# Attention's transfers leave one by one behind ScalarE's operations, and the first expert's weights in halves

## Chip, cores and metric

The kernel runs on one core of a Trainium2 chip. The metric is device time in microseconds, the median of several runs. A trace belongs to one profiled execution, whose span (first to last instruction) is a little shorter than that execution's own time.

## What is computed

Attention over 8 batches and 8 heads, with 512 local and 32 global positions of dimension 64. A local query sees the local keys within 32 positions and all global keys; a global query sees everything. The 4608 rows of 512 then go through a mixture of 16 experts in 4 groups, one expert per row.

```python
s_ll = np.where(np.abs(pos[:, None] - pos[None, :]) <= 32, scale * q_l @ k_l.T, -1e9)
a_l = sm(concat([scale * q_l @ k_g.T, s_ll]))
out_l = a_l @ concat([v_g, v_l])
out_g = sm(scale * q_g @ k_all.T) @ v_all
x = rows of (out_g, out_l)                      # 4608 x 512
g = argmax(x @ w_group); e = argmax(x @ w_expert[g])
out[row] = softmax weights of g and e * (relu(x[row] @ w1[g, e]) @ w2[g, e])
```

## The kernel before

The kernel has two stages. **Attention** walks a list of 40 items, numbered by `n`: for each batch `b` four tiles of 128 local queries, (b, 0) to (b, 3), and one item (b, 'g') for the global queries. Within batches 0 to 6 the global item comes last, so item 4 is (0, 'g') and item 5 is (1, 0). **The experts** follow: for each of 16 experts rows are gathered, multiplied by split weights and scattered.

The order of the engines in attention is written out by hand in the loop over `items` (L920 on); items overlap. In a pass `n` the loop emits, for the item itself, the first half of the scores on TensorE (`scores(it, 0)`, tile `s_ps`), its softmax (`softmax(it, 0)`: VectorE adds the mask into `pr` and takes the minimum, ScalarE takes the exponential, L388), the second half of the scores and of the softmax, and the transposes and the copy of the first half (`transp`, `pt_copy(it, 0)`, ScalarE, L419). For item n-1 it emits the second copy, the products with V (`pv`, tile `x_ps`, L438) and the division (`norm`, into `xbuf`, name `xb`). For items n-2 and n-3 it emits the router's products (`xtrans`, `lt_mm`, `sel_mm`, tiles `xt` and `lm`) and the store `put_x(n-3)`. GpSimd copies windows of V (`make_v`, tiles `vw`) and scatters token numbers (`put`, into `ids_d`).

All direct transfers leave on SyncE's queue (SP) in the order in which the loop emits them. One that has to wait, for a free buffer or for its data, holds those behind it. There are eight semaphores for them, DMAHW0 to DMAHW7, used in turn, so that a transfer also waits until the one eight places ahead has landed. In pass `n` SP gets, all at the head of the pass and before any compute of it:

- `put_x(n-3)`: 256 KB of `xb` to `x_all` (four pieces of 16 KB for a global item), L759 or L464
- `load_q(n+2)`: 256 KB (128 KB for a global item) into one of three buffers (`qz`, or in `kv`), L232
- pieces of the next batch's K (384 KB each, four a batch, into `k_odd` or `kv`, L238) and V (260 KB each and one of 130 KB, six a batch, L247 and L249); batch 1's come in passes 2 to 5
- from two passes after the first expert is known, one 512 KB piece of its first weights (`raw`) in each of four passes, and in passes 35 to 38 one of its second weights (into `kv`), L143

SP isn't tied to the pass in which a transfer is written: it sends as soon as the wait of the transfer allows.

Of the kernel before, what the change touches and what calls it, by code (L numbers as in the profile page):

```python
# [14 lines left out]
AF = mybir.ActivationFunctionType  # L15
# [55 lines left out]
def build(ctx, tc, qT, kT, vU, w1, w2, mask, ca, cb, out):  # L71
# [60 lines left out]
    perm = []  # L132

    def load_w(e, part, ii=range(4), behind=None):
        if e >= NE:
            return
        for i in ii:
            if part == 0:
                hf, c2 = divmod(i, 2)
                src = w1r[ds(perm[e], 1), :, 2 * c2:2 * c2 + 2, hf * 512:(hf + 1) * 512]  # L140
            else:
                src = w2r[ds(perm[e], 1), :, 2 * i:2 * i + 2, :]
            ins = SP.dma_start(out=raws[4 * part + i], in_=src.rearrange("o p c f -> (o p) c f"))  # L143
            if behind is not None:
                tc.add_manual_dep(ins.ins, behind.ins.name,
                                  mybir.DependencyInfo(mybir.DependencyClass.Sync, mybir.DependencyReason.DATA),
                                  reason="paced behind compute")
                behind = None

# [86 lines left out]

    def load_k(b, p):
        SP.dma_start(out=kbuf(b)[:, p, :], in_=kT[b, :, p, :])  # L238

# [3 lines left out]

    def load_v(b, ss):
        for s in ss:
            if s < 5:
                SP.dma_start(out=v0[b % 2][:, s, :], in_=vU[b, 128 * s:128 * s + 128, :])  # L247
            else:
                SP.dma_start(out=v0[b % 2][64:128, s, :], in_=vU[b, 640:704, :])  # L249

# [110 lines left out]
    def softmax(it, i):  # L361
# [3 lines left out]
        if t == 'g':  # L365
            if i:
                return
            mx = sm.tile([128, 2, 2], F32, name="gmx")
            nm = sm.tile([128, 2], F32, name="gnm")
            V.tensor_reduce(mx[:, :, 0], s_ps[:, :, 0:480], AX.X, ALU.max)  # L370
            V.tensor_reduce(mx[:, :, 1], g_ps.rearrange("p (h c) -> p h c", h=2), AX.X, ALU.max)
            V.tensor_reduce(nm, mx, AX.X, ALU.max)
            V.tensor_scalar(nm, nm, -0.125, None, ALU.mult)
            for h in range(2):
                A.activation(pg[h][:, 704:768], g_ps[:, 64 * h:64 * h + 64], AF.Exp, bias=nm[:, h:h + 1], scale=0.125)
            for h in range(2):
                A.activation(pg[h][:, 0:640].rearrange("p (a c) -> p a c", c=128)[:, :, 0:96],
                             s_ps[:, h, 0:480].rearrange("p (a c) -> p a c", c=96), AF.Exp, bias=nm[:, h:h + 1], scale=0.125)
            return
        if i == 0:  # L380
# [3 lines left out]
        for h in range(4 * i, 4 * i + 4):  # L384
            par, p = h % 4 // 2, 2 * i + h % 2
            V.tensor_tensor_reduce(out=pr[:, h, :], in0=s_ps[:, par, 128 * p:128 * p + 128], in1=mask_sb[:, t, :], scale=-0.125, scalar=3.0e38, op0=ALU.add,  # L386
                                   op1=ALU.min, accum_out=nm[:, h:h + 1])
            A.activation(pr[:, h, :], pr[:, h, :], AF.Exp, bias=nm[:, h:h + 1], scale=-1.0)  # L388

# [18 lines left out]
    def pt_copy(it, i):  # L408
# [3 lines left out]
        if t == 'g':  # L412
            V.tensor_copy(ptg[:, i, 0:3, :], tp[0])
            A.copy(ptg[:, i, 3:6, :], tp[1])
            return
# [3 lines left out]
        A.copy(dst, tp)  # L419

# [331 lines left out]

    def put_x(it):
        b, t = it
# [3 lines left out]
        r0 = b * S + SG + 128 * t  # L758
        SP.dma_start(out=x_all[r0:r0 + 128, 0:DM], in_=xbuf[b][:, t, :])  # L759

# [70 lines left out]

    def fetch():
        perm.append(nc.values_load(first_i[0:1, 0:1], engines=(mybir.EngineType.SP,), min_val=0, max_val=NE - 1))
        load_w(0, 0, (0,))

# [76 lines left out]
    def at(n, f, *a):  # L912
        if 0 <= n < len(items):
            f(items[n], *a)

# [4 lines left out]
    for n, it in enumerate(items):  # L920
        now[0] = n
        at(n - 3, put_x)
        if n:
# [3 lines left out]
        b1 = n // 5 + 1  # L927
        if b1 == 1:
            for p in ((), (), (0, 1), (2,), (3,))[n]:
                load_k(1, p)  # L930
            load_v(1, ((), (), (), (0, 1), (2, 3))[n])
        elif b1 < B:
            for p in ((0, 1), (2,), (3,), (), ())[n % 5]:
                load_k(b1, p)
            load_v(b1, ((), (0,), (1,), (2, 3), (4, 5))[n % 5])
        if n == 5:
            load_v(1, (4, 5))
        if chosen and n == chosen[0] + 2:
            fetch()
        elif chosen and chosen[0] + 2 < n < chosen[0] + 6:  # L940
            load_w(0, 0, (n - chosen[0] - 2,))
        if n == 31:
            early_id()
        if 35 <= n < 39:
            load_w(0, 1, (n - 35,))
        while stores and stores[0][0] <= n:
# [27 lines left out]
        if it[1] != 'g':  # L974
            rt_at(n - 2, lt_mm)
        softmax(it, 1)
        at(n - 1, norm)
# [5 lines left out]
        if it[1] == 'g':  # L983
            rt_at(n - 2, lt_mm)
        pt_copy(it, 0)
        if it[1] == 'g':
# [562 lines left out]
```

## Time and profile before

| | us |
|---|---|
| median of 3 runs | 745.93 (745.5 to 746.29) |
| the profiled execution | 743.79 |
| its span | 742.0 |
| TensorE busy | 677.9 (91% of the span) |
| VectorE, ScalarE, GpSimd busy | 410.5, 386.7, 252.0 |

Attention takes about the first 255 us, the experts the rest. The share of busy time is an average over both; what bounds a stretch is read from that stretch. An idle time put down to "issue" is one in which the engine waited for nothing that the profile shows: all semaphores that the next instruction needs were there. The DMA views list the queues: q1 carries the direct transfers that SP issues, q0 GpSimd's indirect ones, q8 and q14 instructions.

### The profile page before, as it was taken

The page shows a single profiled execution, that of the slowest core. Times are in us where ns is not written, and L with a number is a line of the kernel's source. Part 1 is how long each engine was busy: PE and PEld are TensorE (multiplying, and loading weights), DVE is VectorE, ACT ScalarE, POOL GpSimd, SP SyncE. Part 2 cuts the span into 40 slices and gives each one's busy share as a digit, 9 for nine tenths or more (in the row PEclk, how much of TensorE's full clock was granted, in tenths as well). Part 3 has the DMA queues.
Part 4 walks back from the last instruction along what each step waited for, and adds up shares of the span by engine and source line. Part 5 has one row for each costly group of instructions (what it writes and reads, how often), then busy time and mean ns, then how long its engine had stood idle before and what let it go on. Part 6 is the DMA issues. An engine that isn't in the chain of part 4 may idle for free. (4 is left out here: it accounts for less than half of the span.)

```text
span 742.0 us, 24040 instructions
## 1 busy us (share of the span) xinstructions
PE 677.9 (91%) x8891; PEld 532.2 (72%) x8891; DVE 410.5 (55%) x1360; ACT 386.7 (52%) x835; POOL 252.0 (34%) x309
## 2 busy tenths in 40 slices
PE   6889888897887989999989999999999999897996
PEld 3666566575665687767779888867886798786964
DVE  3568667686777725634265455426435563656642
ACT  4676676674757425533355344435335454545642
POOL 5534454455444463212321231232122213323211
PEclk9999999998999999999999999999999999998999
DMA  9876675676662156445348447423834464575730
GB/s 297 239 217 214 187 220 159 193 216 192 207 201 79 35 165 223 154 134 198 118 147 285 153 151 251 152 98 117 294 118 157 141 230 160 179 273 172 253 135 27
DMA packets 76279, 132.47 MB, mean 179 GB/s; under 512 B 17310, under 2 KB 21286, under 8 KB 75952
## 3 DMA queue, kind: packets, MB, share of 16 engines
q1 hardware_dynamic: 66512, 110.92, 45.9%
q0 software_dynamic: 9440, 17.94, 7.5%
q8 instruction: 113, 1.85, 1.1%
q14 instruction: 214, 1.75, 0.8%
HBM read 119.07 MB, written 19.04 MB: 186 GB/s over the span
## 5 line engine op out<-in xcount | busy, mean ns | idle before, releaser
L1183 POOL DMA_INDIRECT xg<-x_all,ids x61 | 72.5, 1189 | 249.4 <-PE yp L1252 48.6
L172 DVE TENSOR_TENSOR w1l<-raw,w1h 128x1024 fp32r<-128x1024 f32 x44 | 51.9, 1221 | 112.2 <-ACT w1h L171 112.2
L388 ACT ACTIVATE pr<-pr,nm 128x128 f32<-128x128 f32 x256 | 81.9, 391 | 48.2 <-DVE nm L386 47.9
L60 POOL COPY vw<-v 32x520 f32<-32x520 f32 (+1 forms) x112 | 69.1, 619 | 87.2 <-DMA ids_d<-cb_sb,si 44.8
L386 DVE CUSTOM_DVE_ANT_0 pr<-s_ps,mask_sb 128x128 f32<-128x128 f32 x256 | 59.0, 286 | 40.9 <-PE s_ps L357 38.6
L1277 PE MATMUL h_ps<-xTh,w1h 128*128 128x256 f32 (+5 forms) x216 | 69.5, 334 | 0.0
L1278 PE MATMUL h_ps<-xTh,w1l 128*128 128x256 f32 (+5 forms) x216 | 68.9, 331 | 0.0
L171 ACT CAST w1h<-raw 128x1024 fp32r<-128x1024 f32 x44 | 43.9, 1047 | 39.1 <-issue 39.1
L1290 DVE SCALAR_TENSOR_TENSOR hTl<-h_ps,hTh 128x256 fp32r<-128x256 f32 (+3 forms) x54 | 28.9, 535 | 56.0 <-ACT hTh L1289 50.9
L1266 PE MATMUL yqp<-w2h,hTh 128*128 128x512 f32 x128 | 52.8, 412 | 7.7 <-issue 7.7
L172 DVE TENSOR_TENSOR w2l<-kv,w2h 128x1024 fp32r<-128x1024 f32 x35 | 42.6, 1223 | 25.8 <-ACT w2h L171 17.6
L1252 PE MATMUL yp<-w2h,hTh 128*128 128x512 f32 x136 | 54.8, 403 | 0.6 <-ACT yr L1246 0.6
L1254 PE MATMUL yp<-w2h,hTl 128*128 128x512 f32 x136 | 53.9, 396 | 0.0
L1253 PE MATMUL yp<-w2l,hTh 128*128 128x512 f32 x136 | 53.9, 396 | 0.0
L1266 PE MATMUL yqp<-w2l,hTh 128*128 128x512 f32 x128 | 51.6, 403 | 0.0
L1289 ACT ACTIVATE hTh<-h_ps 128x256 fp32r<-128x256 f32 (+3 forms) x54 | 25.5, 472 | 46.8 <-PE h_ps L1283 40.2
L419 ACT COPY pt<-t_ps 128x512 f32<-128x512 f32 x64 | 36.8, 575 | 22.9 <-PE t_ps L405 22.7
L438 PE MATMUL x_ps<-v,pt 128*32 128x65 f32 x768 | 44.9, 228 | 4.1 <-ACT pt L419 2.9
L438 PE MATMUL x_ps<-vw,pt 128*32 128x65 f32 x1280 | 44.9, 228 | 2.4 <-ACT pt L419 1.1
L1283 PE MATMUL h_ps<-xTl,w1h 128*128 128x256 f32 (+5 forms) x216 | 45.4, 332 | 0.0
L1269 ACT ACTIVATE y<-yp,gt 128x512 f32<-128x512 f32 x17 | 11.7, 690 | 63.5 <-PE yp L1254 63.5
L405 PE MATMUL t_ps<-ident,pr 128*128 128x128 f32 x256 | 42.7, 290 | 1.7 <-issue 1.7
(259 smaller groups left out, 1647.0 us busy)
## 6 DMA issues: line engine op xcount, KB each, us to landing
raw<-w SPq DMA_DIRECT2D x64, 512.0 KB
kv<-w SPq DMA_DIRECT2D x64, 512.0 KB
v<-vU SPq DMA_DIRECT2D x40, 260.0 KB
x_all<-xb SPq DMA_DIRECT2D x32, 256.0 KB
k_odd<-kT SPq DMA_DIRECT2D x16, 384.0 KB
kv<-qT SPq DMA_DIRECT2D x21, 256.0 KB
kv<-kT SPq DMA_DIRECT2D x12, 384.0 KB
qz<-qT SPq DMA_DIRECT2D x11, 256.0 KB
```

Of the source, the lines that this page charges most:

```text
L60: r = op(*a, **k)
L172: V.tensor_tensor(lo, src, hi.bitcast(F32), ALU.subtract)
L386: V.tensor_tensor_reduce(out=pr[:, h, :], in0=s_ps[:, par, 128 * p:128 * p + 128], in1=mask_sb[:, t, :], scale=-0.125, scalar=3.0e38, op0= ...
L388: A.activation(pr[:, h, :], pr[:, h, :], AF.Exp, bias=nm[:, h:h + 1], scale=-1.0)
L438: P.matmul(x_ps[32 * jj:32 * jj + 32, i, DV * (h % 4):DV * (h % 4) + DV], d['pt'][:, hp, 32 * jj:32 * jj + 32], wins[(b,) + win(4 * t + jj ...
L1183: return G.indirect_dma_start(out=dst, out_offset=None, in_=x_all, in_offset=bass.IndirectOffsetOnAxis(ap=ix.bitcast(U32), axis=0), bounds ...
L1252: P.matmul(yp, hT[0][:, f, sl], w2h[f], start=(f == 0), stop=False)
L1253: P.matmul(yp, hT[0][:, f, sl], w2l[f], start=False, stop=False)
L1254: P.matmul(yp, hT[1][:, f, sl], w2h[f], start=False, stop=(f == 7))
L1266: P.matmul(yqp, hT[i][:, f, sl], w, start=(k == 0), stop=(k == 23))
L1277: P.matmul(hp[:, sl], w1h[par][:, c, fs], xT[0][:, c, sl], start=(c == 0), stop=False)
L1278: P.matmul(hp[:, sl], w1l[par][:, c, fs], xT[0][:, c, sl], start=False, stop=False)
```

## The change

A helper `pace(ins, behind)` makes a transfer wait for an operation of an engine. `softmax` and `pt_copy` now return their last ScalarE operation. In a pass `n`:

- `load_q(n+2)` stays at the head.
- V and K pieces, and weights, are put into a list `more`. `send(1, ...)` takes one out behind the exponentials of the item's first half, one behind those of the second half (not in a global item), and `send(9, ...)` all that is left behind `pt_copy(it, 0)`.
- `put_x(n-3)` comes behind `pt_copy(n-1, 1)`; in a global item it comes at that place without a wait on ScalarE.
- A 512 KB piece of the first expert's weights becomes two of 256 KB (`load_w_half`), in the same passes as before.
- Batch 1's pieces stay in passes 2 to 5, at the new places.

```diff
+    def pace(ins, behind):
+        if behind is not None:
+            tc.add_manual_dep(ins.ins, behind.ins.name,
+                              mybir.DependencyInfo(mybir.DependencyClass.Sync, mybir.DependencyReason.DATA),
+                              reason="paced behind compute")
+    def load_w_half(i, c, behind):
+        if i < 4:
+            hf, c2 = divmod(i, 2)
+            src = w1r[ds(perm[0], 1), :, 2 * c2 + c, hf * 512:(hf + 1) * 512]
+        else:
+            src = w2r[ds(perm[0], 1), :, 2 * (i - 4) + c, :]
+        pace(SP.dma_start(out=raws[i][:, c, :], in_=src.rearrange("o p f -> (o p) f")), behind)
...
     for n, it in enumerate(items):
         now[0] = n
-        at(n - 3, put_x)
         if n:
             at(n + 2, load_q)
...
+        ks, vs = ((), (), (0, 1), (2,), (3,))[n] if b1 == 1 else (), ((), (), (), (0, 1), (2, 3))[n] if b1 == 1 else ()
+        if 1 < b1 < B:
+            ks, vs = ((0, 1), (2,), (3,), (), ())[n % 5], ((), (0,), (1,), (2, 3), (4, 5))[n % 5]
+        more = [lambda g, s=s: load_v(b1, (s,), g) for s in vs]
+        more += [lambda g, p=p: load_k(b1, p, g) for p in ks]
         if n == 5:
-            load_v(1, (4, 5))
+            more.insert(0, lambda g: load_v(1, (4, 5), g))
...
+            more += [lambda g, i=n - chosen[0] - 2, c=c: load_w_half(i, c, g) for c in range(2)]
...
+            more += [lambda g, i=4 + n - 35, c=c: load_w_half(i, c, g) for c in range(2)]
...
         if it[1] == 'g':
             at(n - 1, pt_copy, 1)
-            softmax(it, 0)
+            send(1, softmax(it, 0))
...
+            at(n - 3, put_x)
         else:
-            softmax(it, 0)
-            at(n - 1, pt_copy, 1)
+            send(1, softmax(it, 0))
+            mid = at(n - 1, pt_copy, 1)
+            at(n - 3, put_x, mid)
...
-        softmax(it, 1)
+        mid = softmax(it, 1)
+        if mid is not None:
+            send(1, mid)
...
-        pt_copy(it, 0)
+        send(9, pt_copy(it, 0))
```

On TensorE, VectorE and ScalarE the instructions stand in the same order before and after; on GpSimd two copies change places with two scatters at one point. Only SP's queue is reordered, with new waits.

SP, passes 18 and 19 (items (3, 3) and (3, 'g')), before: a store, a load of q, then two pieces of V (`v_0_152`), twice.

```order
L759 DMA x_all<-xb_184 128x512 [waits DMAHW0_49,DVE_49]
L232 DMA qz_149<-qT 128x512 [waits DMAHW1_49,PE_49]
L247 DMA v_0_152<-vU 128x520 [waits DMAHW2_49,Pool_49]
L247 DMA v_0_152<-vU 128x520 [waits DMAHW3_49,Pool_49]
L759 DMA x_all<-xb_184 128x512 [waits DMAHW4_49,DVE_49]
L232 DMA kv<-qT 128x512 [waits DMAHW5_49,PE_49]
L247 DMA v_0_152<-vU 128x520 [waits DMAHW6_49,Pool_49]
L249 DMA v_0_152<-vU 64x520 [waits DMAHW7_49,Pool_49]
```

The same two passes after:

```order
L243 DMA qz_149<-qT 128x512 [waits DMAHW0_49,PE_49]
L258 DMA v_0_152<-vU 128x520 [waits DMAHW1_49,Activation_49,Pool_49]
L771 DMA x_all<-xb_184 128x512 [waits DMAHW2_49,DVE_49,Activation_49]
L258 DMA v_0_152<-vU 128x520 [waits DMAHW3_49,Activation_49,Pool_49]
L243 DMA kv<-qT 128x512 [waits DMAHW4_49,PE_49]
L258 DMA v_0_152<-vU 128x520 [waits DMAHW5_49,Activation_49,Pool_49]
L771 DMA x_all<-xb_184 128x512 [waits DMAHW6_49,DVE_49]
L260 DMA v_0_152<-vU 64x520 [waits DMAHW7_49,Activation_49,Pool_49]
```

The load of q now leads, the store stands between the pieces of V, and the pieces wait for ScalarE (`Activation`).

SP, passes 4 and 5 (items (0, 'g') and (1, 0)), before; the fourth piece of batch 1's K is the `k_odd` row, and a name `v_1_153` is batch 1's V:

```order
L759 DMA x_all<-xb_183 128x512 [waits DMAHW2_49,DVE_49]
L232 DMA kv<-qT 128x512 [waits DMAHW3_49,PE_49]
L238 DMA k_odd<-kT 128x768 [waits DMAHW4_49]
L247 DMA v_1_153<-vU 128x520 [waits DMAHW5_49]
L247 DMA v_1_153<-vU 128x520 [waits DMAHW6_49]
L759 DMA x_all<-xb_183 128x512 [waits DMAHW7_49,DVE_49]
L232 DMA kv<-qT 128x512 [waits DMAHW0_49,PE_49]
```

After:

```order
L243 DMA kv<-qT 128x512 [waits DMAHW2_49,PE_49]
L258 DMA v_1_153<-vU 128x520 [waits DMAHW3_49,Activation_49]
L771 DMA x_all<-xb_183 128x512 [waits DMAHW4_49,DVE_49]
L258 DMA v_1_153<-vU 128x520 [waits DMAHW5_49,Activation_49]
L249 DMA k_odd<-kT 128x768 [waits DMAHW6_49]
L243 DMA kv<-qT 128x512 [waits DMAHW7_49,PE_49]
L258 DMA v_1_153<-vU 128x520 [waits DMAHW0_49,Activation_49]
```

The piece of K stands behind two pieces of V, the second of which waits for the last copy of the pass.

TensorE in pass 5, the second half of the scores of item (1, 0), which reads the third and the fourth piece of K, after:

```order
L368 MATMUL s_ps<-k_odd,qz_149 32x128 [waits DMAHW1_49,DVE_49]
L368 MATMUL s_ps<-k_odd,qz_149 32x128 x7
L368 MATMUL s_ps<-k_odd,qz_149 32x128 [waits DMAHW6_49]
L368 MATMUL s_ps<-k_odd,qz_149 32x128 x7
L444 MATMUL x_ps<-v_0_152,gb 32x65 x20
```

Its ninth matmul waits for that same transfer (DMAHW6), as it did before (there DMAHW4).

## Rows read from the trace of the kernel before

**Rows 1.** The page: its head, and of the DMA queues the one with the larger instruction packets (packets, MB, share of 16 engines).

```profile
span 742.0 us, 24040 instructions
...
q8 instruction: 113, 1.85, 1.1%
```

**Rows 2.** Busy time by stretch: us of the span, its length, busy us (and instructions) of PE, PEld, DVE, ACT and POOL, the granted clock, the DMA engines' share, GB/s.

```profile
30.00:225.00 195.00, 168.54 (x5094) 121.52 (x5087) 138.86 (x767) 129.58 (x369) 92.92 (x136) 0.97 0.66 199
...
255.00:742.00 487.00, 462.27 (x2832) 378.53 (x2831) 238.18 (x403) 221.55 (x377) 129.37 (x119) 0.99 0.51 172
```

**Rows 3.** Who waited for whom, TensorE's matmuls, 15 to 242 us: us in total, times, longest us.

```profile
PE s_ps L357 <- issue: 5.9, 6, 1.9
PE t_ps L399 <- ACT gb L377: 5.0, 8, 1.7
...
PE lm L350 <- issue: 3.0, 1, 3.0
PE x_ps L438 <- issue: 1.9, 4, 0.8
PE t_ps L405 <- issue: 1.7, 2, 1.0
...
PE lm L489 <- issue: 1.4, 1, 1.4
PE x_ps L432 <- issue: 1.2, 1, 1.2
PE s_ps L344 <- issue: 1.1, 2, 0.8
```

**Rows 4.** The timeline of TensorE around 108 us: start, us, and in brackets the idle time before and its cause.

```profile
107.92 0.41 PE L405 MATMUL t_ps<-ident,pr 128*128 128x128 f32 x2
109.29 0.44 PE L405 MATMUL t_ps<-ident,pr 128*128 128x128 f32 x2 [0.96 <-issue]
```

**Rows 5.** The DMA view of 106.9 to 107.9 us, of its list of queues the instruction queue (packets, MB, share).

```profile
q8 instruction: 1, 0.02, 5.5%
```

**Rows 6.** The timeline of SP's queue, passes 18 and 19: start, us of the issue.

```profile
102.50 0.33 SPq L759 DMA_DIRECT2D x_all<-xb  x1
102.93 0.38 SPq L232 DMA_DIRECT2D qz<-qT  x1
103.40 0.89 SPq L247 DMA_DIRECT2D v<-vU  x2
107.20 0.33 SPq L759 DMA_DIRECT2D x_all<-xb  x1
107.62 0.60 SPq L232 DMA_DIRECT2D kv<-qT  x1
108.31 0.41 SPq L247 DMA_DIRECT2D v<-vU  x1
```

**Rows 7.** The timeline of TensorE at its longest such gap.

```profile
168.85 0.44 PE L350 MATMUL lm<-k_odd,qg 128*32 128x64 f32 x15
172.28 0.22 PE L350 MATMUL lm<-k_odd,qg 128*32 128x64 f32 x1 [2.98 <-issue]
```

**Rows 8.** The DMA view of 168 to 169.7 us: its list of queues holds q1, below, and q0, and no instruction queue.

```profile
q1 hardware_dynamic: 219, 0.42, 91.5%
```

**Rows 9.** The DMA view of 169.7 to 171 us, the instruction queue.

```profile
q8 instruction: 1, 0.02, 5.6%
```

**Rows 10.** Busy time by stretch, columns as in Rows 2: ahead of a q8 packet that a gap of TensorE follows. Eight such stretches were read; these are the quiet one, ahead of the gap of 1.4 us, and of the other seven the highest DMA share, the lowest, and that ahead of the longest gap.

```profile
83.00:84.00 1.00, 1.00 (x55) 0.62 (x40) 0.70 (x7) 0.62 (x3) 0.00 (x0) 1.00 0.12 33
...
105.00:107.00 2.00, 1.83 (x76) 1.38 (x76) 1.74 (x11) 2.00 (x8) 0.61 (x1) 1.00 0.99 293
...
139.10:141.10 2.00, 2.00 (x107) 1.46 (x95) 0.83 (x8) 1.21 (x4) 1.66 (x4) 1.00 0.79 248
167.80:169.80 2.00, 1.49 (x33) 0.47 (x32) 1.57 (x3) 1.11 (x4) 0.19 (x1) 1.00 0.96 257
```

**Rows 11.** Busy time by stretch, the same columns: behind the gaps at 17 and at 169 us.

```profile
19.00:22.00 3.00, 3.00 (x63) 2.33 (x63) 0.93 (x8) 1.86 (x6) 2.46 (x4) 0.68 1.00 307
22.00:25.00 3.00, 1.91 (x68) 1.33 (x64) 1.68 (x11) 1.64 (x5) 0.00 (x0) 0.75 0.61 222
...
174.00:180.00 6.00, 5.01 (x113) 3.68 (x103) 3.51 (x13) 2.68 (x7) 1.46 (x3) 0.50 0.49 183
```

**Rows 12.** The timeline of ScalarE in pass 18: exponentials of the first half, the copy of item 17, those of the second half, the copy of the item.

```profile
107.90 1.28 ACT L388 ACTIVATE pr<-pr,nm 128x128 f32<-128x128 f32 x4 [0.40 <-DVE nm L386]
109.77 0.59 ACT L419 COPY pt<-t_ps 128x512 f32<-128x512 f32 x1 [0.59 <-PE t_ps L405]
...
111.63 1.28 ACT L388 ACTIVATE pr<-pr,nm 128x128 f32<-128x128 f32 x4 [0.79 <-DVE nm L386]
...
112.96 0.58 ACT L419 COPY pt<-t_ps 128x512 f32<-128x512 f32 x1
```

**Rows 13.** The timeline of SP's queue, the fourth piece of batch 1's K.

```profile
26.10 0.44 SPq L238 DMA_DIRECT2D k_odd<-kT  x1
```

**Rows 14.** The timeline of ScalarE in pass 4: the last exponentials, and the copy.

```profile
34.32 1.22 ACT L377 ACTIVATE gb<-s_ps,gnm 128x480 f32<-128x480 f32 x2
35.95 0.48 ACT L414 COPY gb<-t_ps 128x384 f32<-128x384 f32 x1 [0.41 <-PE t_ps L399]
```

**Rows 15.** The timeline of TensorE in pass 5: the second half of the scores of item (1, 0).

```profile
38.22 0.67 PE L357 MATMUL s_ps<-k_odd,qz 64*32 64x128 f32 x32
```

More of the change, by code (lines that the diff above doesn't have):

```diff
@@ L143, in load_w @@
             ins = SP.dma_start(out=raws[4 * part + i], in_=src.rearrange("o p c f -> (o p) c f"))
[L144 to L148, printed above, removed]
+            pace(ins, behind)
+            behind = None
+    def load_w_half(i, c, behind):
[5 more added lines that the diff above has]
+        pace(SP.dma_start(out=raws[i][:, c, :], in_=src.rearrange("o p f -> (o p) f")), behind)
     def fill(e, part, m, S=V):
@@ L235, in kbuf, with load_k @@
         return k_odd if b % 2 else kv[:, 0:KW].rearrange("p (a c) -> p a c", a=4)
-    def load_k(b, p):
-        SP.dma_start(out=kbuf(b)[:, p, :], in_=kT[b, :, p, :])
+    def load_k(b, p, behind=None):
+        pace(SP.dma_start(out=kbuf(b)[:, p, :], in_=kT[b, :, p, :]), behind)
     v0 = [vp.tile([128, 6, VW], F32, name=f"v0_{i}") for i in range(2)]
@@ L242, in build, with load_v @@
         G.memset(t_[0:64, 5, :], 0.0)
-    def load_v(b, ss):
+    def load_v(b, ss, behind=None):
         for s in ss:
             if s < 5:
-                SP.dma_start(out=v0[b % 2][:, s, :], in_=vU[b, 128 * s:128 * s + 128, :])
+                pace(SP.dma_start(out=v0[b % 2][:, s, :], in_=vU[b, 128 * s:128 * s + 128, :]), behind)
             else:
-                SP.dma_start(out=v0[b % 2][64:128, s, :], in_=vU[b, 640:704, :])
+                pace(SP.dma_start(out=v0[b % 2][64:128, s, :], in_=vU[b, 640:704, :]), behind)
     wins = {}
@@ L413, in pt_copy @@
             V.tensor_copy(ptg[:, i, 0:3, :], tp[0])
-            A.copy(ptg[:, i, 3:6, :], tp[1])
-            return
+            return A.copy(ptg[:, i, 3:6, :], tp[1])
         if i == 0:
@@ L418, in pt_copy @@
         dst = d['pt'][:, 4 * i:4 * i + 4, :].rearrange("p a c -> p (a c)")
-        A.copy(dst, tp)
+        return A.copy(dst, tp)
     def pv(it, i):
@@ L751, in patch, with put_x @@
         put(2)
-    def put_x(it):
+    def put_x(it, behind=None):
         b, t = it
@@ L758, in put_x @@
         r0 = b * S + SG + 128 * t
-        SP.dma_start(out=x_all[r0:r0 + 128, 0:DM], in_=xbuf[b][:, t, :])
+        pace(SP.dma_start(out=x_all[r0:r0 + 128, 0:DM], in_=xbuf[b][:, t, :]), behind)
     def choose():
@@ L913, in at @@
         if 0 <= n < len(items):
-            f(items[n], *a)
+            return f(items[n], *a)
     def rt_at(n, f, *a):
@@ L927, in build @@
         b1 = n // 5 + 1
[L928 to L935, printed above, removed]
+        ks, vs = ((), (), (0, 1), (2,), (3,))[n] if b1 == 1 else (), ((), (), (), (0, 1), (2, 3))[n] if b1 == 1 else ()
[3 more added lines that the diff above has]
+        more += [lambda g, p=p: load_k(b1, p, g) for p in ks]
         if n == 5:
-            load_v(1, (4, 5))
+            more.insert(0, lambda g: load_v(1, (4, 5), g))
         if chosen and n == chosen[0] + 2:
-            fetch()
-        elif chosen and chosen[0] + 2 < n < chosen[0] + 6:
-            load_w(0, 0, (n - chosen[0] - 2,))
+            fetch_id()
+        if chosen and chosen[0] + 2 <= n < chosen[0] + 6:
+            more += [lambda g, i=n - chosen[0] - 2, c=c: load_w_half(i, c, g) for c in range(2)]
         if n == 31:
@@ L944, in build, with send @@
         if 35 <= n < 39:
-            load_w(0, 1, (n - 35,))
+            more += [lambda g, i=4 + n - 35, c=c: load_w_half(i, c, g) for c in range(2)]
+        def send(k, behind):
+            for _ in range(k):
+                if more:
+                    more.pop(0)(behind)
         while stores and stores[0][0] <= n:
```

13 lines of the change are left out of this document (7 added, 6 removed).

## The prediction

> **What bounds the kernel now.** I read the busy times by stretch first [rows 2]. The change touches attention only, the first 255 us; the experts, 487 us at 95% of TensorE, get the same instructions and loads. In attention's steady part, 30 to 225 us, TensorE is busy 168.5 of 195 us, VectorE 138.9 and ScalarE 129.6: TensorE leads, and its 26.5 us of idle time are what a better order can win there. The DMA engines are busy 0.66 of that time: no bound on average.
>
> Next I asked whom TensorE waited for [rows 3]. The largest cause is none of the engines: "issue", 5.9 + 3.0 + 1.9 + 1.7 + 1.4 + 1.2 + 1.1 = 16.2 us in 17 gaps between 15 and 242 us. (ScalarE's global softmax is next, 5.0 us.) No wait on q, K or V is in the list: the loads are all early.
>
> A gap seen closely: TensorE stops between the second and the third of four equal transposes at 108.33 and goes on at 109.29 [rows 4], so neither data nor buffers hold it. A packet of the instruction queue q8 runs between 106.9 and 107.9 [rows 5]; q8's packets are 1.85 MB / 113 = 16.4 KB each [rows 1]. At the longest gap TensorE stops at 169.3 between the fifteenth and the sixteenth of sixteen equal matmuls [rows 7]; up to 169.7 no instruction packet ran [rows 8], then one did [rows 9], and TensorE went on 1.3 us after 171. I read the gaps as TensorE running out of instructions: the next block came late. Ahead of seven of eight such blocks the DMA engines were 0.79 to 0.99 busy [rows 10], against the mean of 0.66 [rows 2], and at 108 us SP had just sent its batch: four transfers, 256 + 256 + 260 + 260 KB, from 102.50 to 104.3, the next batch from 107.20 on [rows 6]. At the 293 GB/s of [rows 10] those 1032 KB are 3.6 us of work handed over in 1.8 us. A block that is asked for then stands behind up to 2 us of loads.
>
> [...]
>
> **The change, part by part.**
>
> *Spacing (the main term).* ScalarE's points in pass 18 are at 107.90 + 1.28 = 109.2, 109.77 + 0.59 = 110.4, 111.63 + 1.28 = 112.9 and 112.96 + 0.58 = 113.5 us [rows 12]. There leave V, the store, V, and the next q. That is two pairs of some 516 KB, 1.8 us of work each, 3.1 us apart, in place of four in a row. When the second of a pair leaves, about 1 us is queued, not 2. Placing all transfers of passes 2 to 39 on these points of the traced run, at 290 GB/s, I estimate (from all such rows of SP and ScalarE, of which [rows 6, 12] are one pass) that the time with over 1.5 us of queued work falls from 21% to 10%, and the queue that a block finds from 1.0 to 0.6 us on average. I take 60% of the gaps as gone: 0.6 x 16.2 = 9.7 us. The ends are 40% (the time with over 1 us queued falls only from 36% to 24%, and in passes with weights three transfers still leave together behind the last copy) and 85%.
>
> *What of it reaches the end.* A gap of TensorE is a loss only where it would not have waited anyway. With 86% busy it mostly would not, but its work is tied to VectorE and ScalarE item by item, and half of its 26.5 idle us are waits on these, which close part of a gap. I take 70%, with 50% and 100% as ends: 6.8 us (3.2 to 13.8).
>
> *The clock behind a gap.* [...] After the 1.9 us gap at 17 us it was 0.68 and 0.75 for 6 us: 3.0 x 0.32 + 1.9 x 0.25 = 1.4 us [rows 11]. Together 3.9 us; I take half, 2.0 (0 to 3.9).
>
> *Lateness.* SP's queue ran up to a pass ahead of compute; now each piece waits for its own pass. K and V of a batch are still sent over the five passes before it, so nearly all have more than one pass of 5 to 6 us to spare, and q stays at the head. Batch 1 is the exception: its loading starts only in pass 2. Its fourth piece of K left at 26.10 [rows 13]; now it stands behind the last copy of pass 4, which ends at 35.95 + 0.48 = 36.4 [rows 14]. V, the store and V, 776 KB since 35.5, are ahead: 2.7 us, so 38.3; its own 384 KB take 1.3 us, so 39.6 at the earliest. TensorE wants it half-way through the scores that began at 38.22 [rows 15], at about 38.5. A new wait of 1.1 us at least, some 3 us if a landing costs 2 us more; I take 2.0. Moving the other K pieces past V and the stores costs nothing by the same count: whole passes of compute cover them. Without that cover the price is a wait of this kind in each batch, 2 us x 7.
>
> *Halves, waits, the rest.* Eight issues of 0.4 us more on SP, which sends some six transfers in a pass of 5 to 6 us: covered by SP's idle time. In halves a load of weights puts 0.9 us of work ahead of others at a time, not 1.8 us. The waits stand on SP alone; behind each are only later transfers. ScalarE, VectorE and TensorE get no instruction. The stores move half a pass; their buffers are reused two batches later. The swap of two copies on GpSimd is worth one scatter at most, and GpSimd is 48% busy. The last weights (passes 35 to 38) leave up to two passes later, still in passes before ScalarE converts them.
>
> Sum: -6.8 - 2.0 + 2.0 = -6.8 us (ends -16.6 and -0.2). The traced execution took 743.79, so 737.0; the median of the runs shown is 2.1 us higher, so 745.93 - 6.8 = 739.1, say **739.0**.
>
> **Rivals.**
>
> *The block waits for a turn, not for the queue.* If an instruction packet only waits until the running packets end, the depth of SP's queue is nothing to it, only whether the engines are busy counts, and 0.66 of the time they are, before and after. The gaps then stay and just move; the K piece costs 2.0: 747.9, or 745.9 where a moved gap swallows it. For it: one of the gaps (1.4 us, `lm` L489 [rows 3]) follows a stretch in which the DMA engines were 0.12 busy [rows 10], and pairs of transfers still fill the engines. Against it: the packet that came only after 169.7, when loads had been queued for microseconds [rows 8, 9], and the 0.79 to 0.99 ahead of the other seven that I read.
>
> [...]
>
> *Late data, slower.* The K wait of pass 5 is not 2 but 3 us, the clock falls behind it as it did at 17 us (1.4 us), and the gaps give back less than these 4.4 us. Price: up to +4.4, 750.3; with a small gain from the gaps about 748.5. It decides if less than a third of the 13.6 us (9.7 + 3.9) comes back. For it: 39.6 against 38.5 is worked out with no allowance for landing. Against it: it happens once, and a late block fell just there in any case (1.2 us in `x_ps` L432 [rows 3]).
>
> *All gaps go.* Two pairs may be short enough that every block comes in time: -13.8 - 3.9 + 1.1 = -16.6, 729.3.
>
> **How the numbers follow.** Forecast (some 733 to 744) 0.65; all gaps go 0.07; turn 0.16; late data 0.12. A measurement of this kernel tells about 0.2%, 1.5 us, from no change: faster means below 744.4, slower above 747.4. Forecast and "all gaps" give 0.70 faster (0.02 of the forecast's lower part is no gain); the turn gives 0.11 same and 0.05 slower, late data 0.03 same and 0.09 slower. So 0.70, 0.16, 0.14. The range leaves a tenth out on either side: 730.5 to 747.5.
>
> **What would show it.** Right: "issue" on TensorE from 15 to 242 us falls from 16.2 to about 6.5 us; the gap of 3 us with weights and K in flight is gone and the clock behind it stays at 1.00; attention is 5 to 9 us shorter and the experts are as long as before; a wait on `k_odd` appears once, near 38 us, of 1 to 3 us; SP waits mainly for ScalarE. Wrong: the "issue" total stays near 16 us although SP's transfers are spaced; or waits on `kT`, `vU` or `qT` show up in more than one batch; or the gaps go and the waits of TensorE on ScalarE and VectorE grow by as much, so that attention is no shorter.

## The result, and the profile after

The change makes the kernel **slower**: 750.88 us median (747.28 to 756.20, 12 runs) against 745.71 for the kernel before on the same chip (738.90 to 746.60, 12 runs). The ratio is 1.0104, 95% interval 1.0066 to 1.0142. It is that of the means, 751.5 and 743.7: seven executions of the kernel before took 745.5 to 746.6 us and five 738.9 to 742.9, which its median doesn't show. The forecast was 739.0, with 730.5 to 747.5 as its range. Ratios leave out slow executions (over 1.5% above the fastest of their kernel), so in the tables below, too, they need not be the quotient of the medians.

The profiled execution took 747.28 us, which is the fastest of the twelve; a second one, taken later, took 756.93 and is used below. The page of the first, its head and the queue of the larger instruction packets (packets, MB, share of 16 engines):

```profile
span 745.4 us, 24126 instructions
...
q8 instruction: 113, 1.85, 1.1%
```

The packets of this queue are as many as before, 113 [rows 1]. Whom TensorE waited for, 15 to 242 us (us in total, times, longest us):

```profile
PE s_ps L368 <- issue: 9.8, 11, 1.4
PE t_ps L412 <- ACT gb L388: 6.3, 8, 1.7
PE s_ps L368 <- DVE nm L398: 4.8, 7, 1.1
PE s_ps L368 <- DMA k_odd<-kT: 3.7, 1, 3.7
PE xt_ps L485 <- DVE xb L470: 3.5, 8, 0.9
...
PE x_ps L444 <- issue: 2.0, 3, 1.4
PE x_ps L450 <- issue: 1.8, 5, 0.7
```

"Issue" is 9.8 + 2.0 + 1.8 = 13.6 us in 19 gaps, against 16.2 us in 17 [rows 3]. The longest is 1.4 us, where it was 3.0; but there are more of them, and the total that was to fall to 6.5 has hardly moved. A wait of 3.7 us on a piece of K is new. The SP queue did what the diff says (15 to 242 us, the three largest waits):

```profile
SPq L258 <- ACT pr L400: 27.4, 21, 2.5
SPq L258 <- ACT gb L388: 24.7, 6, 4.9
SPq L249 <- ACT pr L400: 23.4, 11, 8.0
```

Busy time by stretch (columns as in Rows 2), with the two stretches of [rows 2] first, then the K wait and what follows it:

```profile
30.00:225.00 195.00, 164.45 (x5020) 119.19 (x5020) 138.50 (x752) 127.00 (x360) 94.17 (x138) 0.99 0.72 205
255.00:742.00 487.00, 463.47 (x2842) 379.31 (x2840) 239.60 (x407) 222.19 (x379) 128.70 (x119) 0.99 0.51 171
...
37.00:40.70 3.70, 0.01 (x1) 0.00 (x0) 0.00 (x0) 0.83 (x2) 3.06 (x6) 0.92 0.98 293
...
41.00:44.00 3.00, 3.00 (x120) 2.52 (x104) 0.93 (x8) 1.28 (x4) 2.46 (x4) 0.58 0.46 141
```

The experts, as foretold, run as before. In attention TensorE is at another place when such a window of 195 us opens and closes (5020 matmuls, before 5094), so equal work is compared further down. The DMA engines are busy 0.72 of it, before 0.66. From 37 to 40.7 us TensorE stands still while the DMA engines are 0.98 busy, and for 3 us behind that its granted clock is 0.58: 0.50 up to 43.5 us, 0.97 in the half us from there.

The wait itself. The timeline of SP (start, us of the issue) around batch 1's fourth piece of K, and that of TensorE:

```profile
33.91 0.33 SPq L258 DMA_DIRECT2D v<-vU  x1
34.33 0.92 SPq L771 DMA_DIRECT2D x_all<-xb  x1
35.34 0.39 SPq L258 DMA_DIRECT2D v<-vU  x1
35.78 0.42 SPq L249 DMA_DIRECT2D k_odd<-kT  x1
36.29 0.41 SPq L243 DMA_DIRECT2D kv<-qT  x1
37.02 0.33 SPq L258 DMA_DIRECT2D v<-vU  x1
37.40 0.50 SPq L260 DMA_DIRECT2D v<-vU  x1
```

```profile
36.56 0.45 PE L368 MATMUL s_ps<-k_odd,qz 64*32 64x128 f32 x16
40.75 0.68 PE L368 MATMUL s_ps<-k_odd,qz 64*32 64x128 f32 x16 [3.74 <-DMA k_odd<-kT]
```

The piece left at 35.78 us and TensorE went on at 40.75, between the sixteenth and the seventeenth of 32 records (two for each of the program's 16 matmuls), half-way, where the forecast had put it; in the kernel before the 32 ran through [rows 15]. What that did to the pass is read from ScalarE's exponentials of item (1, 0) and of item (1, 1):

```profile
35.71 1.28 ACT L400 ACTIVATE pr<-pr,nm 128x128 f32<-128x128 f32 x4 [0.77 <-DVE nm L398]
...
45.84 1.28 ACT L400 ACTIVATE pr<-pr,nm 128x128 f32<-128x128 f32 x4 [0.48 <-DVE nm L398]
```

The same two in the kernel before:

```profile
37.37 1.28 ACT L388 ACTIVATE pr<-pr,nm 128x128 f32<-128x128 f32 x4 [0.77 <-DVE nm L386]
...
43.83 1.28 ACT L388 ACTIVATE pr<-pr,nm 128x128 f32<-128x128 f32 x4 [0.48 <-DVE nm L386]
```

After, they are 10.13 us apart; before, 6.46: the pass took 3.67 us more, from 1.66 us ahead to 2.01 behind.

From there to the end this execution loses only some 1.4 us more. From the first exponentials of item (1, 1) to those of item (7, 3), 4985 records of matmuls in every trace, it isn't slower at all; first the kernel before, then the changed one (columns as in Rows 2):

```profile
43.83:235.72 191.89, 165.13 (x4985) 119.36 (x4983) 138.53 (x765) 128.57 (x365) 94.08 (x136) 0.97 0.63 191
```

```profile
45.84:237.55 191.71, 162.73 (x4985) 117.57 (x4983) 140.19 (x765) 129.06 (x366) 91.22 (x132) 1.00 0.70 197
```

TensorE is idle 2.2 us more (28.98 against 26.76) and busy 2.4 us less, at a granted clock of 1.00 where it was 0.97. So the clocks of these two executions hide a loss. The median execution is 3.6 us longer than the profiled one (750.88 against 747.28), so this trace alone can't show the whole loss. The experiments had to.

### The profile page after: what moved, and what is told of

Same layout as the page of the kernel before. It is cut to its first block, busy times and chain, and to the rows that moved or that the text cites. A ratio compares the mean times of both kernels' runs of the same rounds, so it can differ in the third digit from the quotient of the medians.

```text
span 745.4 us, 24126 instructions
## 1 busy us (share of the span) xinstructions
PE 674.8 (91%) x8891; PEld 529.8 (71%) x8891; DVE 412.4 (55%) x1360; ACT 386.7 (52%) x835; POOL 251.2 (34%) x309
## 5 line engine op out<-in xcount | busy, mean ns | idle before, releaser
L182 ACT CAST w1h<-raw 128x1024 fp32r<-128x1024 f32 x44 | 43.9, 1047 | 37.9 <-issue 35.7
L1294 PEld LDWEIGHTS h_ps<-xTh,w1h 128*128 128x128 f32 x216 | 40.5, 188 | 3.2 <-issue 0.8
```

Source lines behind the costliest of these rows:

```text
L1294: P.matmul(hp[:, sl], w1h[par][:, c, fs], xT[0][:, c, sl], start=(c == 0), stop=False)
```

## Experiments

Five groups of runs were made. Ratios are against the kernel before in the same group on the same chip, with a 95% interval; its median was 745 to 751 us from group to group, so times of different groups are not compared. "Issue" is TensorE's total from 15 to 242 us, in one profiled execution.

### First group: which part costs?

**e1_batch1_early**: the changed kernel, batch 1's pieces back at the head of the pass, without waits.

```diff
-        more += [lambda g, p=p: load_k(b1, p, g) for p in ks]
+        lk = [lambda g, p=p: load_k(b1, p, g) for p in ks]
+        more = lk + more if b1 == 1 else more + lk
...
+        if b1 == 1:
+            for f in more:
+                f(None)
+            more = []
```

> The changed kernel, but batch 1's pieces of K and V leave at the head of passes 2 to 5 without a wait on ScalarE, as before the change; all else stays paced. Late data (the one wait of 3.7 us on K in pass 6 with what follows it is the loss): the wait is gone and the time is 4 to 5 us under the changed kernel, about 746, equal to before. Lateness harmless, the spacing of the steady batches is the loss: stays at 749 to 751, although the wait is gone. My forecast's spacing gain, hidden under the late piece: below 743.

**e2_batch1_late**: the kernel before, batch 1's pieces alone behind ScalarE.

```diff
-            for p in ((), (), (0, 1), (2,), (3,))[n]:
-                load_k(1, p)
-            load_v(1, ((), (), (), (0, 1), (2, 3))[n])
+            more = [lambda g, s=s: load_v(1, (s,), g) for s in ((), (), (), (0, 1), (2, 3))[n]]
+            more += [lambda g, p=p: load_k(1, p, g) for p in ((), (), (0, 1), (2,), (3,))[n]]
...
```

> The kernel before, but only batch 1's pieces of K and V wait for ScalarE's operations of their passes; all later transfers as before. Late data: one wait on K of 3 to 4 us appears and the time is 3 to 5 us above before, 749 to 750. Spacing of the steady batches as the cause: within 1.5 us of before.

**e3_whole_weights**: the changed kernel with weights in pieces of 512 KB.

```diff
-            more += [lambda g, i=n - chosen[0] - 2, c=c: load_w_half(i, c, g) for c in range(2)]
+            more += [lambda g, i=n - chosen[0] - 2: load_w(0, 0, (i,), g)]
...
```

> The changed kernel, but the first expert's raw weights leave in pieces of 512 KB, at the places of the first halves. If the halves cost or save anything: 1 to 2 us either way. Late data or spacing as the cause: the same as the changed kernel within 1.5 us, 749 to 752.

**e4_order_only**: the changed kernel's order on SP, without the waits on ScalarE in attention.

```diff
-    def pace(ins, behind):
-        if behind is not None:
+    def pace(ins, behind, keep=False):
+        if behind is not None and keep:
...
```

> The changed kernel without its waits on ScalarE in attention: the transfers stand on SP's queue in the changed order, but each leaves as soon as its buffer and its data allow. Late data: the fourth piece of batch 1's K leaves early again, the wait is gone, and the time is 4 to 5 us under the changed kernel, about 746. If it is the order itself (q ahead of the stores, V ahead of K) that loses: 749 to 751.

| | us | ratio | interval |
|---|---|---|---|
| the kernel before | 750.94 | | |
| e1, batch 1 early | 756.22 | 1.0071 | 1.0040 to 1.0102 |
| e2, only batch 1 late | 752.35 | 1.0020 | 0.9991 to 1.0050 |
| e3, whole weights | 756.18 | 1.0071 | 1.0032 to 1.0110 |
| e4, order without waits | 751.82 | 0.9986 | 0.9949 to 1.0022 |

The wait on K is there in e2 and gone in e1. By itself it costs 0.2%, which can't be told from nothing; without it the change is still 0.7% slower. The new order costs nothing. Halves aren't the cause either: without them the loss is as large. What is left are the waits on ScalarE from batch 2 on, called the hold below: a transfer that could leave is held until an engine has come to a given operation. The wait of TensorE in e2:

```profile
PE s_ps L363 <- DMA k_odd<-kT: 3.7, 1, 3.7
```

### Second and third group: what in the hold?

**e5_pass_earlier**: e1 with K and V from batch 2 on sent one pass earlier, still behind ScalarE. It asks whether data come late. The edit of the two lists:

```diff
-        if 1 < b1 < B:
-            ks, vs = ((0, 1), (2,), (3,), (), ())[n % 5], ((), (0,), (1,), (2, 3), (4, 5))[n % 5]
+        elif n < 34:
+            b1 = (n + 1) // 5 + 1
+            ks, vs = ((0, 1), (2,), (3,), (), ())[(n + 1) % 5], ((), (0,), (1,), (2, 3), (4, 5))[(n + 1) % 5]
...
```

> The kernel of e1 (batch 1 early, all else paced as in the change), but from batch 2 on each piece of K and V leaves one pass earlier, behind ScalarE's operations of the pass before. Lateness (GpSimd's window copies and then TensorE get V too late in every batch): the loss of e1, 0.7%, is gone, within 0.3% of before. The waits themselves (a queue that is held at ScalarE's points uses the DMA engines no better, and instruction blocks come as late as before): 0.5 to 1% slower than before, as e1.

**e6_no_kv_before** and **e7_no_kv_after**: the kernel before, and the changed one, without the loads of K and V from batch 2 on. They ask whether these loads make the gaps; later batches then use old K and V, rows go to other experts, and only attention is read. The edit of e6 (in e7 the condition is `1 < b1 < B`):

```diff
-        elif b1 < B:
+        elif 0:
```

> The kernel before, without the loads of K and V from batch 2 on: batches 2 to 7 use the K and V of batches 0 and 1, so rows go to other experts and only attention's stretch and the ratio to e7 are to be read. If blocks of instructions stand behind loads: issue gaps of TensorE between 60 and 220 us fall from some 11 us to under 4, and attention is 5 to 10 us shorter. If the gaps have nothing to do with loads: as many as before.

> The changed kernel with the same loads left out. If the change loses by what the paced loads of K and V do to the DMA engines or by their lateness: within 0.3% of e6 plus the one wait on batch 1's K, some 4 us. If it loses by waits that stay without these loads (stores and weights behind ScalarE): more than 6 us above e6.

**e8_kv_paced_only**: the kernel before with only K and V from batch 2 on behind ScalarE, at the changed kernel's points.

```diff
-            for p in ((0, 1), (2,), (3,), (), ())[n % 5]:
-                load_k(b1, p)
-            load_v(b1, ((), (0,), (1,), (2, 3), (4, 5))[n % 5])
+            more += [lambda g, s=s: load_v(b1, (s,), g) for s in ((), (0,), (1,), (2, 3), (4, 5))[n % 5]]
+            more += [lambda g, p=p: load_k(b1, p, g) for p in ((0, 1), (2,), (3,), (), ())[n % 5]]
...
```

> The kernel before, but K and V from batch 2 on wait for ScalarE's operations as in the change; batch 1, stores and weights as before. If the pacing of K and V is the loss: 0.5 to 1% slower than before. If stores or weights are: within 0.3%.

**e9_one_point_first**: e8 with all pieces of a pass in a row behind the first exponentials. **e10_one_point_last**: all behind the last copy. They undo the spacing and keep the hold. The edit of e9 (e10 drops these calls of `send` and keeps that behind the last copy):

```diff
-            send(1, softmax(it, 0))
+            send(9, softmax(it, 0))
...
```

> The kernel of e8, but all pieces of K and V of a pass leave in a row behind the exponentials of the item's first half. If the spacing loses (each piece starts with the DMA engines empty and they are busy longer for the same bytes): within 0.3% of before. If holding them at ScalarE loses, whatever the spacing: 0.5 to 1% slower, as e8.

> The kernel of e8, but all pieces of K and V of a pass leave in a row behind the last copy of the pass. By the spacing: within 0.3% of before. By the hold: 0.5 to 1% slower. If the two points differ by over 0.5%, the place within the item counts, not spacing or hold.

**e11_changed_again** and **e12_before_again**: the two kernels as they are, no edit.

> The changed kernel once more, for a second trace and its ratio beside those of e9 and e10: 0.7 to 1.4% slower than before; issue gaps of TensorE of 10 to 15 us.

> The kernel before once more, against itself: the ratio is 1 within 0.3%, which bounds what the other ratios can tell; a second trace of before shows how far issue gaps (12.8 us in the first, over the items from (1, 1) to the last) vary by themselves: 9 to 14 us.

| | us | ratio | interval |
|---|---|---|---|
| the kernel before, beside e5 and e8 | 749.55 | | |
| the kernel before, beside the others | 750.17 | | |
| e5, a pass earlier | 759.45 | 1.0109 | 1.0067 to 1.0151 |
| e8, only K and V held | 755.68 | 1.0064 | 1.0032 to 1.0097 |
| e9, all at the first point | 755.45 | 1.0069 | 1.0030 to 1.0109 |
| e10, all at the last point | 756.06 | 1.0075 | 1.0044 to 1.0106 |
| e11, the change again | 759.97 | 1.0133 | 1.0094 to 1.0172 |
| e12, before against itself | 748.43 | 0.9998 | 0.9965 to 1.0031 |

Holding K and V behind ScalarE costs 0.64 to 0.75% (e8, e9, e10), however it is done. Spread over three points or all at one is the same: **spacing, on which the forecast's gain rested, is worth nothing that shows.** (The intervals are of some 0.4% to either side; the forecast had 0.9%.) More lead doesn't help (e5), so from batch 2 on it isn't lateness.

e6 and e7 answer the other half. TensorE's issue waits, 15 to 242 us, of e6:

```profile
PE x_ps L438 <- issue: 3.7, 5, 2.4
PE s_ps L357 <- issue: 2.7, 8, 0.5
PE x_ps L432 <- issue: 1.4, 4, 0.5
PE t_ps L399 <- issue: 0.7, 1, 0.7
```

And of e7:

```profile
PE x_ps L450 <- issue: 3.1, 10, 0.4
PE s_ps L368 <- issue: 2.6, 3, 2.0
PE x_ps L444 <- issue: 0.4, 1, 0.4
```

8.5 us without K and V where it was 16.2, and 6.1 where it was 13.6. What is left is of another kind. The DMA packets of the traces show it: in the kernel before, 16 of the 17 gaps end 1.2 to 1.6 us after a packet of q8 ended, as at 109.29 us [rows 4, 5], and in all twenty traces every gap of 0.8 us or more did, 128 of them. Call a gap that ends 1.1 to 1.7 us behind such a packet a block gap. From 50 us on, block gaps come to 11.8 us in the kernel before and 11.4 after, but to 0.0 in e6 and 0.4 in e7; what stays there are short gaps of 0.7 us at most, nearly all at other distances from a packet; their cause is open. So with these loads go nearly all of the block gaps, and their being there counts, not how they are spread. (One execution each.)

Yet attention, which was to be 5 to 10 us shorter in e6, is not: the stretch of equal work took 191.89 us in the kernel before. From the first exponentials of item (1, 1) to those of item (7, 3), e6:

```profile
43.39:236.46 193.07, 166.90 (x4985) 120.02 (x4983) 139.10 (x765) 128.24 (x366) 94.36 (x136) 0.98 0.36 103
```

And e7:

```profile
44.05:231.35 187.30, 162.15 (x4985) 117.64 (x4983) 137.01 (x765) 128.38 (x366) 95.05 (x137) 1.00 0.37 105
```

In this stretch "issue" falls from 13.1 to 6.1 us (the kernel before, e6), but idle time only from 26.8 to 26.2: other waits take the place of the gaps, those of `s_ps` on VectorE 2.1 to 5.5 us, of `x_ps` on ScalarE 3.0 to 5.0. From the changed kernel to e7 "issue" falls by 8.0 us and idle time by 3.8. Stores and weights behind ScalarE, which e7 keeps, show no cost here.

Where a usual execution of the change loses, e11 against e12 shows. The same stretch, first e12, the kernel before:

```profile
39.90:233.61 193.71, 163.66 (x4985) 118.36 (x4983) 138.31 (x765) 128.74 (x365) 94.91 (x136) 1.00 0.63 189
```

And e11, the changed kernel:

```profile
46.07:246.09 200.02, 169.12 (x4985) 122.13 (x4983) 139.63 (x765) 129.42 (x366) 94.93 (x136) 0.97 0.66 188
```

It starts 6.2 us late and takes 6.3 us longer (4.4 us more, behind it, are not explained). Of the 6.3, 5.5 us are busy time of TensorE, and 169.12 x 0.97 = 164.0 us at full clock is about what e12 needed: the matmuls are the same, the clock is lower. The other 0.8 us are idle time. The runs say so too: the mean granted clock was 0.972 to 0.981 in the six of e11, 0.983 to 0.995 in those of e12. In e8, where K and V alone are held, it isn't so: 0.986 on average, as the kernel before beside it, so the loss of e8 isn't the clock. The DMA engines are busy 0.66 for 188 GB/s, where 0.63 moved 189. (e12's profiled execution, 739.98 us, is its fastest, and e11's, 756.93, too.) e11 also has the K wait, 5.0 us this time.

### Fourth and fifth group: ScalarE's points, or any hold?

By then two theories were left: that ScalarE's points cost by their *place* (they fall just ahead of TensorE's dense runs of scores and products with V, where 5.9 + 1.9 + 1.2 + 1.1 = 10.1 of the 16.2 us of issue gaps stood [rows 3]), or that *any hold* costs.

**e13_behind_dense**: e8, the pieces behind TensorE where such runs end. **e14_ahead_of_dense**: the same, just ahead of them. First the points of e13, then those of e14 (ScalarE's are dropped in both):

```diff
-        scores(it, 0)
+        send(1, scores(it, 0))
...
-        at(n - 1, pv, 1)
+        send(9, at(n - 1, pv, 1))
...
```

```diff
-        at(n - 1, transp, 1)
+        send(1, at(n - 1, transp, 1))
...
-        transp(it, 0)
+        send(9, transp(it, 0))
...
```

> The kernel before with only K and V from batch 2 on held back to their own pass, but behind TensorE in place of ScalarE: the first piece of a pass waits for the last matmul of the first half of the scores, the rest for the last product with V of the second half, so the loads start at the end of TensorE's dense runs of small matmuls. If the place is what costs (loads in flight while a dense run's instructions are fetched): 0.995 to 1.001 of the kernel before, and TensorE's issue gaps from batch 1 on 3 us or more below the 12.8 us of that kernel. If the hold itself costs, wherever it falls: 1.0065 to 1.0075 as behind ScalarE. If a wait on another engine costs: the same 1.0065 to 1.0075.

> The same, with the points moved just ahead of the dense runs: the first piece of a pass waits for the last transpose of the item before, ahead of the products with V, the rest for the last transpose of the item's own first half, ahead of the next scores. If the place is what costs: 1.006 to 1.012, at least 0.6% above the run with the loads behind the dense runs, and more gaps inside scores and products with V. If the hold itself costs: 1.0065 to 1.0075, the same as the other place within 0.3%. If a wait on another engine costs: the same.

**e15_wait_not_binding**: the kernel before; K and V wait for a copy of ScalarE two passes back.

```diff
-                load_k(b1, p)
-            load_v(b1, ((), (0,), (1,), (2, 3), (4, 5))[n % 5])
+                load_k(b1, p, last[n - 2])
+            load_v(b1, ((), (0,), (1,), (2, 3), (4, 5))[n % 5], last[n - 2])
...
```

> The kernel before, its transfers in their old order at the head of the pass, K and V from batch 2 on waiting for the last ScalarE copy of the pass two before, which is done when they leave, so that the wait is there and the times of leaving stay nearly as they were. If the hold or its place costs: 0.998 to 1.002. If the wait on another engine costs: 1.005 to 1.0075.

**e16_all_behind_dense** and **e17_all_ahead_of_dense**: e1 with all its points moved to TensorE, as in e13 and as in e14, the store among them. The first reads:

```diff
-            mid = at(n - 1, pt_copy, 1)
-            at(n - 3, put_x, mid)
+            at(n - 1, pt_copy, 1)
...
-        at(n - 1, pv, 1)
+        last = at(n - 1, pv, 1)
+        at(n - 3, put_x, last)
+        send(9, last)
...
```

> The changed kernel with batch 1's K and V early again (head of the pass, no wait) and all its other points moved to the end of TensorE's dense runs: the first piece of a pass behind the first half of the scores, the store, the other pieces and the weights in halves behind the last product with V. If the place is what costs: 0.995 to 1.002 of the kernel before, 0.5 to 0.9% below the 1.0071 that the same kernel gave with ScalarE's points. If holding the transfers back costs in itself: 1.006 to 1.009.

> The same with all points just ahead of the dense runs: the first piece behind the last transpose of the item before, the store, the other pieces and the weights behind the last transpose of the item's first half. If the place is what costs: 1.004 to 1.010, at least 0.4% above the form behind the dense runs, with TensorE's issue gaps inside scores and products with V 3 us or more above that form's. If holding back costs in itself: 1.006 to 1.009, within 0.3% of the other form.

**e18_kv_behind_scalar**: e8 once more, in the group of e16 and e17.

> Again the kernel before with K and V from batch 2 on behind ScalarE's points, now beside the two forms above. If ScalarE's points cost by their place: 1.004 to 1.008, as it did (1.0064). If its 0.64% was of the chip that it ran on: 0.998 to 1.002, and the place theory loses its main number.

| | us | ratio | interval | issue, us |
|---|---|---|---|---|
| the kernel before, beside e13 to e15 | 745.29 | | | |
| the kernel before, beside e16 to e18 | 744.76 | | | |
| e13, K and V behind dense runs | 745.18 | 0.9993 | 0.9964 to 1.0023 | 12.2 |
| e14, K and V ahead of them | 747.27 | 1.0039 | 1.0005 to 1.0074 | 18.7 |
| e15, a wait long over | 746.67 | 1.0023 | 0.9988 to 1.0059 | 15.6 |
| e16, all behind dense runs | 742.85 | 0.9976 | 0.9944 to 1.0007 | 14.6 |
| e17, all ahead of them | 744.94 | 0.9989 | 0.9952 to 1.0026 | 11.6 |
| e18, K and V behind ScalarE | 747.13 | 1.0047 | 1.0006 to 1.0088 | 19.9 |

e18 repeats the loss, 0.47% this time. "Any hold" doesn't fit: e16 and e17 are e1 with other points, and 1.0071 becomes 0.9976 and 0.9989 (another group, each beside its own kernel before); beside e18 in their own group they hold more transfers than it and lose nothing that shows. Nor do TensorE's points hold for less time. In the traces K's pieces from batch 2 on leave on average 3.4 us after the first exponentials of their pass in e17, as in e18, and 3.3 in e8; V's (those of the global items not counted) 2.4, 2.6 and 2.4. In the kernel before they leave 4.6 and 3.2 us ahead of these exponentials, in e5, which loses more than e1, 2.2 and 3.1 ahead. "Place" fits e13 and e16; e14 has the sign, but at 0.4% not the 0.6 to 1.2% foretold, and the plainest test fails: e17, with everything ahead of the dense runs, was to be 0.4 to 1.0% slower and was not. e15 decides nothing: the wait by itself costs 0.2%, from -0.1 to +0.6.

In these two groups the time goes with the gaps. TensorE's issue waits of e17 (739.22 us in its profiled execution) and of e18 (749.30):

```profile
PE x_ps L454 <- issue: 4.5, 5, 1.2
PE s_ps L369 <- issue: 4.3, 3, 2.3
PE lm L506 <- issue: 2.3, 1, 2.3
...
PE s_ps L355 <- issue: 0.5, 2, 0.3
```

```profile
PE s_ps L363 <- issue: 8.9, 8, 2.0
...
PE lm L496 <- issue: 4.2, 2, 2.5
PE x_ps L445 <- issue: 3.8, 4, 1.7
...
PE s_ps L350 <- issue: 1.7, 2, 0.9
PE lm L356 <- issue: 1.0, 1, 1.0
...
PE t_ps L413 <- issue: 0.3, 1, 0.3
```

11.6 and 19.9 us. The three runs with the fewest idle us of this kind (e17, e13, e16) have ratios of 0.9976 to 0.9993, the three with the most (e15, e14, e18) 1.0023 to 1.0047. By these totals it isn't so elsewhere: e11 has 13.1 us of them and e12 13.7, and e3, 0.7% slower, 11.9. By block gaps from 50 us on it is, within each group: 9.1 and 7.7 us in e1 and e3, which lose, against 5.0 and 3.7 in e2 and e4; 8.4 to 8.7 in e9, e10 and e11 against 5.8 in e12; 8.8, 11.0 and 13.2 in e13, e15 and e14, in the order of their ratios; 14.3 in e18 against 5.8 and 8.0 in e17 and e16. Only the first pair has as many before as after, and e5 and e8 have no kernel without loss beside them (11.5 and 9.7). So the hold behind ScalarE seems to lose by more idle time in block gaps, not less; these are single executions, sorted after the event, and no run was made to test it.

e16 is the best form that was run: 0.24% below the kernel before, with an interval that takes in no change.

## Why the prediction was wrong

*What bounds the kernel.* The reading of the gaps holds as far as the runs go: 16 of the 17 in the kernel before end 1.2 to 1.6 us after an instruction packet, and without the loads of K and V from batch 2 on the block gaps from 50 us on fall from 11.8 us to 0.0 (e6). That TensorE runs out of instructions there stays the author's reading; no trace shows what it has left to issue.

*Spacing* **is the step that failed.** It said that a block waits for the work queued ahead of it, so that two pairs of transfers in place of four in a row take 60% of the gaps away, 9.7 us. The transfers were spaced, and the total stood at 13.6 us in one execution and 13.1 in another (e12, the kernel before, has 13.7; kernels with these loads had 10.2 to 19.9 in single executions). With the spacing undone and the hold kept (e9, e10) the time is the same. The estimate of the queue came from placing transfers on an old trace at 290 GB/s, first come, first served; in the trace after, the DMA engines were busier than before (0.72 against 0.66), not more idle.

*What of it reaches the end.* 70% was taken, and this was too much as well. Between the profiled executions of e17 and e18, 8.3 us of gaps stand against 10.1 us of time, but from the first exponentials of item (1, 1) to those of item (7, 3) it is 6.0 us of gaps against 3.3 us of time (189.46 and 192.74 us). With the loads left out it is 7.0 us of gaps against 0.6 of idle time (e6 and the kernel before; against e12 6.4 and 3.9), and 8.0 against 3.8 (e7 and the changed kernel). This is what the prediction named as a sign of being wrong: the gaps go, and waits on ScalarE and VectorE grow. A tenth to six tenths is what these single executions show.

*The clock behind a gap* was to give 2.0 us back. It went the other way: a new wait brought its own low clock (0.58 for 3.0 us of work, 1.3 us), and in e11 TensorE is busy 5.5 us longer at a lower clock (0.97 against 1.00). No run shows the 3.9 us that the 2.0 are half of: 1.4 of them are counted behind the gap at 17 us, and for the rest there are, from 174 to 180 us, 5.01 us of TensorE's work at a granted clock of 0.50 [rows 11], by the same count 2.5 us.

*Lateness* had the right place and the wrong size. The piece left at 35.78 us (36.4 foretold), but landed 4.9 us later, not 3.2. The count had 776 KB ahead of it, moving at once, and its own 384 KB. But the first of these, which left at 33.91, moved its first packet at 34.86; and of q and V that left behind the piece (256 + 260 + 130 KB) 0.24 MB were through before its last packet ended at 40.33, some 0.8 us of the engines' time (an estimate, at the forecast's 290 GB/s). The up to 2 us that the forecast allowed for a landing were its author's assumption: TensorE went on at 40.75, 0.42 us after that last packet. The packets' sizes tell the transfers apart: those of K are of 3072 bytes. The DMA view from 35.7 to 40.7 us (packets, MB, share; then KB and us to landing):

```profile
q1 hardware_dynamic: 710, 1.43, 95.0%
...
k_odd<-kT SPq DMA_DIRECT2D x1, 384.0 KB, 4.9
```

3.7 us and 1.3 of clock make 5.0, not 2.0.

*Halves, waits, the rest* at nothing: right for the halves as far as e3 tells, and for the order (e4). The waits are the second step that failed: they were put at nothing because only later transfers stand behind them, and there the 0.5 to 0.75% lies (e8, e9, e10, e18). With the 0.2% of the K wait (e2) that is 0.7 to 0.95%, within the interval of the 1.04% measured.

*The rivals.* "Late data, slower" has the sign, nearly the mechanism (a K wait of 3 us and 1.4 of clock foretold) and nearly the time: 748.5 to 750.3 against 750.88. It would be a mistake to stop there. Its wait alone (e2) costs 0.2%, and the change without it (e1) is 0.7% slower. "The block waits for a turn" said that the gaps stay and move, which they did (13.6 us after 16.2), but allowed for 745.9 to 747.9, and no run here shows a turn by itself. "All gaps go" is out. No rival had the loss that e8 shows: K and V held behind ScalarE from batch 2 on.

*What stays open.* Why that hold costs: more time in block gaps, by the traces (14.3 us in e18 against 5.8 and 8.0 in e17 and e16), but not why more. It isn't lead (e5), spacing (e9, e10), the order (e4), or holding as such, or for how long (e16, e17); place on TensorE's run isn't shown (e14 half for it, e17 against). Whether ScalarE and TensorE differ as what is waited for, or only in where their points fall by a fraction of a microsecond, was not tried: it takes a wait on either engine that falls at the same moment.

## What to carry to other kernels

Before spreading transfers out to close issue gaps, leave the transfers out once: that shows how much of the gaps is theirs at all (here 11.8 us of block gaps fell to 0.0), and how much idle time goes with them (26.8 to 26.2 us), which bounds what spacing can win. Then send them all at one point: if the time is the same, spacing is nothing. A load that is tied to compute loses its lead (batch 1's fourth piece of K left at 35.78 us, before at 26.10): check the first batch, whose lead is the shortest, and count what leaves behind a load, too, since some of it may pass (0.24 MB here). A late-data story that matches the measured loss to half a microsecond can still be about a fifth of it; undoing just that part tells.

## Not expected of the hardware

- Transfers moved in the order of leaving, but not strictly: the K piece of 384 KB took 4.9 us to land, and 0.24 MB of those that left after it were through before its last packet.
- A long issue gap of TensorE ended 1.2 to 1.6 us after an instruction packet: so did all 128 of 0.8 us or more. With no K and V loads from batch 2 on, 6.1 to 8.5 us of issue gaps stayed, but hardly one of this kind from 50 us on (0.0 us in e6, 0.4 in e7).
- The kernel before had a median of 750.2 us in one group and of 744.8 in a later one on the same chip, with executions from 738 to 752 us in the latter: more than most effects here, so only ratios within a group were read.
